# The first two chunks of a hash-attention and MLP kernel in another hand-written order

## The chip, the cores and the metric

The kernel runs on one core of one Trainium2 chip. The metric is the device time of one execution in microseconds (us); a kernel's number is the median of several runs. Engines are named as in the profile: PE (TensorE matmuls), PEld (its weight loads), DVE (VectorE), ACT (ScalarE), POOL (GpSimd) and SP (SyncE, which only issues transfers here). The profile is one execution of its own, with its own span.

## The reference

Each of 4 batches has 8 heads of 768 tokens with 64 dimensions. A query may attend only to keys of its own bucket; the bucket is the pattern of signs of six random projections. The outputs of the 8 heads together are one row of 512 values, which goes through a layer norm and a two-layer MLP.

```python
def _attn_ref(q, k, v, proj):
    q_bits = (np.einsum('bhsd,dk->bhsk', q, proj) > 0)      # six signs per token
    k_bits = (np.einsum('bhsd,dk->bhsk', k, proj) > 0)
    ...
    mask = q_bucket[:, :, :, None] == k_bucket[:, :, None, :]
    scores = scale * np.matmul(q, k.transpose(0, 1, 3, 2))
    scores = np.where(mask, scores, -1000000000.0)
    ...                                                     # softmax over keys
    return np.matmul(attn, v)

def _moe_ref(x, g_ln, w_ch1, w_ch2):
    xn = (x - mu) / np.sqrt(var + 1e-06) * g_ln
    ch = np.maximum(xn @ w_ch1, 0.0) @ w_ch2                # 512 -> 2048 -> 512
    return x + ch
```

## The kernel before

**Masking by matmul.** A head's operand in the tile `slots` has 70 rows: 64 rows of the transposed q or k in bf16 and 6 rows of bits, each plus or minus a constant. One matmul over the 70 rows gives the score plus a term that is largest where all six bits agree; the exponential on ACT (line 409) takes that largest value off again, so keys of other buckets come out as zero.

**Chunks and units.** The work is cut into 12 chunks (4 batches, three chunks of 256 queries each). A chunk's attention is 12 units, three for each of four pairs of heads. A unit is four score matmuls into a PSUM tile `sc` (line 403, two buffers), one ACT exponential of 128x1024 into `ex` (line 409, three buffers) and eight matmuls `av` with the values (line 437, two buffers in PSUM). The third unit of a pair ends with two DVE instructions that divide by the sum of weights (lines 452 and 462). For batch 0 the first `av` of a pair is opened by a small matmul (line 428), and `row_sums` (line 354, evicted at 357) prepares its operand.

**How batch 0 is prepared.** There is nothing to hide its preparation behind except its own attention, so the order of the first two chunks is written out by hand in `first_two` (each engine runs its instructions in the order of the program text there). For each head:
- `transposes(h, a)`, line 211: three f32 transposes on PE of q (a=0) or k (a=1) into a PSUM tile; each covers two token blocks, so that 64 partitions hold the even blocks and 64 the odd ones. Line 219 (DVE, q) and line 221 (ACT, k) evict them to the f32 tile `qkT` (four buffers). The PSUM tile is one of two `mm` buffers; for head 1 it is an `sc` buffer.
- `casts(h)`, lines 226 to 231: two casts of 64x768 from `qkT` to bf16 `slots`, even and odd blocks. Heads 0 and 1: one on POOL and one on ACT. Heads 4 and 6: one on POOL and one on DVE. The others: both on DVE.
- `hash_pair(j, a)`, line 306: projects both heads of pair j in f32; line 311 (DVE) turns the sums into bits. After a=1 it copies the bits to the six rows of `slots`, four copies of 6x768 for each pair: pair 0 two on DVE (326), one on ACT (322) and one on POOL (324), the other pairs three on DVE and one on POOL.

`keep_awake` (line 656) issues dummy matmuls. `values` (line 330) casts the v of four heads on POOL. `load_w1` and `load_w2` (lines 560, 567) and the loads of batch 1 (lines 147, 168) are issued by POOL. `narrow` (line 239) casts batch 1's q and k on POOL, `blocks` (line 244) transposes them on DVE.

The loop over `seq` issues, for step i, first the next unit's scores, then the steps that the table `also` names for i, then the values of unit i. Chunks 0 and 1 alternate by pairs of heads (chunk 0 pair 0, chunk 1 pair 0, chunk 0 pair 1 and so on; the last pairs run chunk 0's pairs 2 and 3 first). All of a pair's bits and casts must be there before its first unit.

**From the third chunk on** nothing is in hand order: `interleave` mixes attention units with the MLP of an earlier chunk (lines 519 `hp` and 536 `o`; the hidden values are evicted to `hbuf` at 129 on DVE or 133 on ACT) and with the preparation of later batches, and a scheduler places the instructions of each engine. Among these are `squares` (line 191), eight ACT instructions for each batch that sum squares of q and k, for a safety check at the end.

Of the kernel before, what the change touches and what calls it, by code (L numbers as in the profile page):

```python
# [9 lines left out]
F32 = mybir.dt.float32  # L10
# [4 lines left out]
AF = mybir.ActivationFunctionType  # L15
# [5 lines left out]
Q_SCALE = 2.0**-12  # L21
# [7 lines left out]
def kernel(  # L29
# [11 lines left out]
    nc = tc.nc  # L41
    P = 128

    B, H, S, D = q.shape
    n_bits = proj.shape[1]
# [10 lines left out]
    scale = 1.0 / math.sqrt(D)  # L56
# [9 lines left out]
    proj1 = consts.tile([P, 2, 32], F32)  # L66
# [25 lines left out]
    HS = HC * P  # L92
# [11 lines left out]
    for i in range(2):  # L104
# [8 lines left out]
    ps_sc = main.enter_context(  # L113
        tc.tile_pool(name="ps_sc", bufs=2, space=bass.MemoryType.PSUM)
    )
    ps_av = main.enter_context(
        tc.tile_pool(name="ps_av", bufs=2, space=bass.MemoryType.PSUM)
    )
# [17 lines left out]
    def load_half(b, half):  # L136

        h0 = half * H // 2
        t = {}
        for nm in "qk":  # L140
            t[nm] = nat.tile([P, H // 2, NC, D], F32, tag=f"{nm}nat", name=f"{nm}nat")

        cuts = [[0, 1, 2, 4] if half == 0 else [0, 2, 4], [0, 4], [0, 2, 4], [0, 2, 4]][b]
        for lo, hi in zip(cuts, cuts[1:]):
            for nm, src in (("q", q), ("k", k)):
                eng = nc.gpsimd if b == 1 else nc.scalar if nm == "k" and hi - lo == 1 else nc.sync
                eng.dma_start(
                    out=t[nm][:, lo:hi],
                    in_=src[b, h0 + lo : h0 + hi].rearrange("h (p c) d -> p h c d", p=P),
                )  # L150
        if b == 0 and half == 0:
            nc.scalar.dma_start(out=proj1[0:D, 0, 0:n_bits], in_=proj)

            nc.scalar.activation(wake2[:, 0:1], wake2[:, 1:2], AF.Exp)
            t["v"] = load_values(b, half)
        return t

    def load_values(b, half):
        h0 = half * H // 2
        eng = nc.gpsimd if (b, half) == (1, 0) else nc.sync  # L160
        if (b, half) == (0, 1):

            t = work.tile([P, NH * CT // 2], F32, tag="h", bufs=1, name="vnat1")[
                :, 0 : H // 2 * NC * D
            ].rearrange("p (h c d) -> p h c d", h=H // 2, c=NC)
        else:
            t = nat.tile([P, H // 2, NC, D], F32, tag="vnat", bufs=1, name="vnat")
        eng.dma_start(
            out=t, in_=v[b, h0 : h0 + H // 2].rearrange("h (p c) d -> p h c d", p=P)
        )  # L170
        return t

    class Prep:

# [6 lines left out]
        def load(self, half):  # L181
            self.tiles[half] = load_half(self.b, half)
# [16 lines left out]

            return self.sl[0:D, h, :, par * HS : (par + 1) * HS]  # L200

        def transposes(self, h, a):

            if a == 0:
                self.qkT[h] = work.tile([P, 2, HS], F32, tag="qkT", bufs=4, name="qkT")
            if h == 1:
                tp = ps_sc.tile([P, 2, 512], F32, tag="sc", name="tpose")[:, 0, 0:HS]
            else:
                tp = ps_mm.tile([P, HS], F32, tag="mm", name="tpose")
            for i in range(HC):  # L210
                nc.tensor.transpose(  # L211
                    tp[:, i * P : (i + 1) * P],
                    self.tiles[h // 4]["qk"[a]][:, h % 4, 2 * i : 2 * i + 2].rearrange(
                        "p c d -> p (c d)"
                    ),
                    identf,
                )
            if a == 0:
                nc.vector.tensor_scalar_mul(self.qkT[h][:, a, :], tp, Q_SCALE)
            else:  # L220
                nc.scalar.activation(self.qkT[h][:, a, :], tp, AF.Copy)

        def casts(self, h):
            src = self.qkT[h]
            if h < 2:
                nc.gpsimd.tensor_copy(self.tokens(h, 0), src[0:D])
                nc.scalar.activation(self.tokens(h, 1), src[D:P], AF.Copy)
            else:
                eng = nc.gpsimd if h in (4, 6) else nc.vector
                eng.tensor_copy(self.tokens(h, 0), src[0:D])  # L230
                nc.vector.tensor_copy(self.tokens(h, 1), src[D:P])  # L231

        def narrow(self, half, a):

# [64 lines left out]
        def hash_pair(self, j, a):  # L299

            if a == 0:
                self.pair_bits = work.tile([P, 2, HS], BF16, tag="bits", name="bits")
            bits = self.pair_bits
            hp = ps_mm.tile([P, HS], F32, tag="mm", name="hash")
            for g in range(4):
                nc.tensor.matmul(  # L306
                    hp[32 * g : 32 * (g + 1), :],
                    proj1[:, g % 2, :],
                    self.qkT[2 * j + g // 2][:, a, :],
                )  # L310
            nc.vector.tensor_scalar(  # L311
                bits[:, a, :], hp,
                scalar1=0.0, scalar2=0.5, op0=AOP.is_gt, op1=AOP.subtract,
            )
            if a == 0:
                return
            for g in range(4):
                par = g % 2
                dst = self.sl[D:K1, 2 * j + g // 2, :, par * HS : (par + 1) * HS]
                src = bits[32 * g : 32 * g + n_bits]  # L320
                if g == 2 and j == 0:
                    nc.scalar.activation(dst, src, AF.Copy)
                elif g == 3:
                    nc.gpsimd.tensor_copy(dst, src)
                else:
                    nc.vector.tensor_copy(dst, src)  # L326

        def values(self, half):
            hs = slice(half * H // 2, (half + 1) * H // 2)
# [234 lines left out]
    def load_w2():  # L564
        w2ap = moe_w_ch2.rearrange("(o p) d -> p o d", p=P)
        for n8 in range(0, NH, NH // 2):
            nc.gpsimd.dma_start(
                out=w2_sb[:, n8 : n8 + NH // 2, :], in_=w2ap[:, n8 : n8 + NH // 2, :]
            )
# [61 lines left out]
    prep = preps[0]  # L631
# [4 lines left out]
    units = {n: att_units(*chunks[n], xs[n]) for n in range(3)}  # L636
    mlp = {0: mlp_steps(*chunks[0], xs[0])}

    def head(h):
        prep.transposes(h, 0)  # L640
        prep.transposes(h, 1)
        prep.casts(h)

    def first_two():

        nxt = preps[1]
        prep.load(0)
        prep.load(1)
        prep.load_v(1)
        block_diagonal()  # L650
        nc.sync.dma_start(out=gbc, in_=moe_g_ln.partition_broadcast(P))

        def keep_awake(n):
            tp = ps_mm.tile([P, P], F32, tag="mm", name="wakep")
            for _ in range(n):
                nc.tensor.matmul(tp, wake, wake)  # L656

        keep_awake(26)
        head(0)
        head(1)  # L660
        nc.vector.tensor_copy(proj1[D : 2 * D, 1, 0:n_bits], proj1[0:D, 0, 0:n_bits])
        keep_awake(3)
        prep.hash_pair(0, 0)
        prep.hash_pair(0, 1)
        keep_awake(10)
        prep.values(0)
        load_w1()
        groups = [(0, 0), (0, 1), (1, 0), (1, 1), (2, 0), (3, 0), (2, 1), (3, 1)]
        seq = [(n, 3 * j + g) for j, n in groups for g in range(3)]

        also = {
            0: [lambda: head(2), lambda: prep.values(1)],
            1: [lambda: prep.row_sums(0), lambda: head(3), lambda: nxt.load(0)],
            3: [lambda: prep.hash_pair(1, 0)],
            4: [lambda: prep.hash_pair(1, 1)],
            5: [lambda: head(4), load_w2],
            6: [lambda: head(5)],
            7: [lambda: prep.hash_pair(2, 0)],
            8: [
                lambda: prep.row_sums(1), lambda: prep.hash_pair(2, 1), lambda: nxt.load(1), lambda: nxt.load_v(0),  # L680
            ],
            9: [lambda: head(6)],
            10: [lambda: head(7)],
            11: [lambda: prep.hash_pair(3, 0)],
            12: [
                lambda: prep.hash_pair(3, 1), lambda: nxt.narrow(0, 0), lambda: nxt.narrow(0, 1),
            ],
            14: [lambda: nxt.blocks(0, 0, 0)],
            15: [
                lambda: nxt.blocks(0, 0, 1),  # L690
            ],
            18: [mlp[0][0][1]],
            19: [lambda: nxt.operands(0)],
            22: [mlp[0][3]],
            23: [mlp[0][1][0][1]],
        }
        units[0][0][0]()
        for i, (n, u) in enumerate(seq):
            m, w = seq[i + 1] if i + 1 < len(seq) else (2, 0)
            units[m][w][0]()  # L700
            for f in also.get(i, []):
                f()
            units[n][u][1]()

    plan = {
        2: "K10 H10 N11 B11 V10 W11 | T11 H11 E10 Q00 L20 V11 W20",
# [21 lines left out]
    with tc.manual_schedule():  # L731
        first_two()
# [211 lines left out]
```

## Time and profile before

| what | us |
|---|---|
| median of three runs (lowest, highest) | 325.96 (324.23, 326.18) |
| span of the profiled execution | 325.2 |
| PE busy in the span | 305.4 |
| ACT, DVE, POOL busy | 216.8, 181.4, 83.8 |
| PE busy in the 259 us from 66 us on | 247.93 |

A start in the timeline is counted from the span's first instruction. Where a group has several instructions ("x3"), the duration is from the start of the first to the end of the last; the bracket gives how long the engine had been idle before it and what ended that. A wait in the chain is put down to what ended last.

The stages of the first 66 us, by the first exponential of each pair of heads in the timeline (line 409):

| pair 0 of chunk 0 | pair 1 | pair 2 | pair 3 | first of the third chunk | first hash of batch 1 (line 275) |
|---|---|---|---|---|---|
| 11.99 | 22.72 | 34.07 | 38.68 | 52.06 | 64.38 |

### The profile page before, as it was taken

How to read it: one execution, taken by the hardware profiler on the slowest of the kernel's cores; microseconds unless marked ns; L12 is line 12 of the kernel's file. 1: busy time of each engine (PE TensorE's matmuls, PEld its weight loads, DVE VectorE, ACT ScalarE, POOL GpSimd, SP SyncE). 2: the span in 40 equal slices, each digit the busy share in tenths (PEclk: the TensorE clock that was granted, in tenths of full speed). 3: DMA queues.
4: the chain of work that ended last, by engine and by line, in shares of the span. 5: the costliest groups of instructions: out<-in, count | busy, mean ns of one | idle time of the engine just before them, and what ended most of it. 6: DMA issues, size and time to landing. Idle time of an engine off the chain costs nothing.

```text
span 325.2 us, 7843 instructions
## 1 busy us (share of the span) xinstructions
PE 305.4 (94%) x3249; PEld 225.9 (69%) x3276; DVE 181.4 (56%) x399; ACT 216.8 (67%) x274; POOL 83.8 (26%) x105
## 2 busy tenths in 40 slices
PE   6888899999999999999999999989999999999991
PEld 5655568767758868858768769759679688685750
DVE  1578974483575695446596674534643735446320
ACT  4567687935685886876976866997667568672110
POOL 4546623744032260056082040200200200201000
PEclk9999967999999999999999999999999999999998
DMA  7999996985289469497444552030020200200201
GB/s 225 366 211 301 208 331 110 214 250 135 63 187 262 109 166 204 90 266 241 80 111 85 71 120 50 1 89 12 19 80 2 65 34 2 65 34 15 87 27 46
DMA packets 64875, 40.94 MB, mean 126 GB/s; under 512 B 47184, under 2 KB 59728, under 8 KB 64832
## 3 DMA queue, kind: packets, MB, share of 16 engines
q1 hardware_dynamic: 60368, 31.85, 39.2%
q0 software_dynamic: 4096, 8.13, 10.5%
q8 instruction: 27, 0.44, 0.6%
q10 hardware_dynamic: 368, 0.39, 0.4%
q14 instruction: 16, 0.13, 0.1%
HBM read 27.98 MB, written 6.88 MB: 107 GB/s over the span
## 4 chain that ended last, share of the span: by engine, by line
PE 81%; ACT 9%; DVE 5%; issue 3%; ACTq 0%; DVEq 0%
PE hp L519 25%; PE o L536 21%; PE sc L403 17%; PE av L437 10%; ACT ex L409 4%; PE hash L275 3%; DVE slots L326 2%; PE hash L306 2%; ACT qnat L191 1%; ACT knat L191 1%; PE tpose L211 1%; PE wakep L656 1%; DVE bits L311 1%; ACT hbuf L133 1%; DVE slots L231 1%
## 5 line engine op out<-in xcount | busy, mean ns | idle before, releaser
L409 ACT ACTIVATE ex<-sc,expb 128x1024 bf16<-128x1024 f32 x144 | 159.7, 1114 | 65.7 <-PE sc L403 65.0
L519 PE MATMUL hp<-xnT,w_sb 128*128 128x256 bf16 x768 | 99.0, 273 | 0.3 <-ACT hbuf L133 0.3
L536 PE MATMUL o<-w_sb,hbuf 128*128 128x512 bf16 x357 | 92.4, 379 | 1.9 <-ACT hbuf L133 0.7
L403 PE MATMUL sc<-slots 70*128 70x256 bf16 x576 | 90.0, 278 | 3.3 <-DVE slots L326 2.9
L519 PEld LDWEIGHTS <-w_sb 128*128 128x128 bf16 x768 | 72.4, 98 | 9.6 <-issue 0.6
L437 PEld LDWEIGHTS <-ex 128*128 128x128 bf16 x1152 | 54.4, 99 | 22.6 <-ACT ex L409 9.3
L403 PEld LDWEIGHTS <-slots 70*128 70x128 bf16 x576 | 52.1, 99 | 17.5 <-DVE slots L326 2.7
L437 PE MATMUL av<-vaug,ex 128*128 128x65 bf16 x1152 | 60.8, 196 | 2.6 <-ACT ex L409 2.4
L129 DVE TENSOR_SCALAR hbuf<-hp 128x512 bf16<-128x512 f32 x45 | 31.0, 688 | 49.2 <-PE hp L519 48.4
L536 PEld LDWEIGHTS <-hbuf 128*128 128x128 bf16 x384 | 35.5, 97 | 29.2 <-issue 1.2
L497 POOL TENSOR_SCALAR rs<-mv 128x2 f32<-128x2 f32 x12 | 6.2, 513 | 168.0 <-DVE mv L482 167.9
L133 ACT ACTIVATE hbuf<-hp 128x512 bf16<-128x512 f32 x51 | 30.4, 596 | 21.6 <-PE hp L519 21.4
L541 DVE SCALAR_TENSOR_TENSOR x<-o,rs,x 128x512 f32<-128x512 f32 x24 | 17.8, 741 | 33.3 <-PE o L536 33.3
L462 DVE TENSOR_TENSOR x<-x,rc 128x256 f32<-128x256 f32 x36 | 20.7, 574 | 1.0
L454 DVE TENSOR_SCALAR rc<-av 128x4 f32<-128x4 f32 x36 | 5.7, 158 | 23.6 <-PE av L437 23.6
L483 DVE SCALAR_TENSOR_TENSOR xn<-x,mv,gbc 128x512 bf16<-128x512 f32 x24 | 18.0, 766 | 0.1
L481 DVE BATCH_NORM_STATS2 stats<-x 128x6 f32<-128x512 f32 x24 | 15.4, 678 | 0.2
L330 POOL CAST vaug<-vnat 128x1536 bf16<-128x1536 f32 x8 | 12.2, 1525 | 10.5 <-DMA vnat<-in_v_dram 5.5
L455 DVE TENSOR_TENSOR x<-av,vsum 128x256 f32<-128x256 f32 x36 | 14.9, 413 | 0.0
L191 ACT ACTIVATE knat<-knat 128x768 f32<-128x768 f32 x16 | 13.5, 848 | 0.0
L191 ACT ACTIVATE qnat<-qnat 128x768 f32<-128x768 f32 x16 | 13.5, 844 | 0.0
L239 POOL CAST nat<-qnat 128x1536 bf16<-128x1536 f32 x6 | 9.0, 1501 | 16.7 <-DMA qnat<-in_q_dram 10.7
(79 smaller groups left out, 207.6 us busy)
## 6 DMA issues: line engine op xcount, KB each, us to landing
out_dram<-x SPq DMA_DIRECT2D x24, 256.0 KB
vnat<-in_v_dram SPq DMA_DIRECT2D x7, 768.0 KB
qnat<-in_q_dram SPq DMA_DIRECT2D x11, 384.0 KB
knat<-in_k_dram SPq DMA_DIRECT2D x11, 384.0 KB
w_sb<-in_moe_w_ch_dram POOLq DMA_DIRECT2D x4, 1024.0 KB, 13.7
slots<-slots SPq DMA_DIRECT2D x6, 384.0 KB
qnat<-in_q_dram POOLq DMA_DIRECT2D x2, 768.0 KB, 13.3
knat<-in_k_dram POOLq DMA_DIRECT2D x2, 768.0 KB, 14.6
```

The lines of the kernel that those rows point to most:

```text
L129: nc.vector.tensor_scalar_max(dst, src, 0.0)
L133: nc.scalar.activation(dst, src, AF.Relu if relu else AF.Copy)
L191: nc.scalar.activation(src, src, AF.Square, accum_out=sq[:, a, col : col + 1],)
L403: nc.tensor.matmul(sc[:, i, :], sl[0:K1, h, 1, kj * P : (kj + 1) * P], sl[0:K1, h, 0, q0 : q0 + CT],)
L409: nc.scalar.activation(ex, sc, AF.Exp, bias=expb[:, 1:2] if b else expb[:, 0:1], scale=scale if b else scale / Q_SCALE,)
L437: nc.tensor.matmul(av[:, h - ha, qi, :], state[g][:, i, qi * P : (qi + 1) * P], va[:, h, CMAP[b][kj], :], start=(b > 0 and (g, i, qi) == ( ...
L462: nc.vector.tensor_tensor(xv, num, rc.unsqueeze(3).to_broadcast([P, 2, TT, D]), op=AOP.mult)
L481: nc.vector.bn_stats(stats, x[:, i, :])
L483: nc.vector.scalar_tensor_tensor(xn[:, :, i, :], x[:, i, :].rearrange("p (o d) -> p o d", d=P), mv[:, i, 0:1], gbc.rearrange("p (o d) -> p ...
L519: nc.tensor.matmul(hp[:, i, :], w1_sb[:, dt, nt * P : (nt + 1) * P], st["xnT"][:, dt, :], start=(dt == 0), stop=(dt == ND - 1),)
L536: nc.tensor.matmul(o2, st["h"][:, nt, i * P : (i + 1) * P], w2_sb[:, nt, :], start=(nt == 0), stop=(nt == NH - 1),)
L541: nc.vector.scalar_tensor_tensor(x[:, i, :], o2, st["rs"][:, i : i + 1], x[:, i, :], op0=AOP.mult, op1=AOP.add,)
```

## The change

- The transfer of `proj` is issued by SP, behind head 0's q, and not by ACT behind both k loads. The values of heads 0 to 3 come as two transfers (heads 0 and 1 ahead of q and k of heads 2 and 3, heads 2 and 3 behind them), and the POOL cast of them as two, `pair_values`.
- `keep_awake(3)` and `keep_awake(10)` go; the 26 dummy matmuls at the start stay.
- `casts` becomes `cast` with an engine for each half. Heads 2 to 7: all on DVE. Head 0: DVE and ACT. Head 1: POOL and ACT, as before.
- The four bit copies become a step of their own, `bit_rows`, all on DVE.
- The transposes of heads 2 and 3 stand before the first scores, into an `sc` and the two `av` buffers, evicted by ACT and DVE (head 2 both by ACT). Those of heads 4 and 5 stand at steps 4 and 5, with their casts at 6 and 7; those of heads 6 and 7 at 9 and 10. Before, each head's transposes and casts were one step.
- `values(1)`, batch 1's loads, `load_w2`, `row_sums(1)`, `narrow` and `blocks` keep their order among themselves and move by zero to two steps.

From the end of `seq` on, PE has the same instructions in the same order in both kernels, and DVE and POOL too. In the third chunk the order on ACT and SP differs. ACT before: `hbuf`, square of q, exponential, `hbuf`, square of q, `hbuf`, square of k, `hbuf`, exponential, `hbuf`, square of k, `hbuf`, exponential. ACT after: `hbuf`, both squares of q, exponential, square of k, `hbuf`, square of k, `hbuf`, `hbuf`, exponential, `hbuf`, `hbuf`, exponential. On SP one load of batch 2's q stands ahead of the second transposing transfer of batch 1, not behind it.

```diff
+            if (b, half, hi) == (0, 0, 1):
+                nc.sync.dma_start(out=proj1[0:D, 0, 0:n_bits], in_=proj)
+            if (b, half, hi) == (0, 0, 2):
+                t["v"] = load_values(b, half, 0, 2)
         if b == 0 and half == 0:
-            nc.scalar.dma_start(out=proj1[0:D, 0, 0:n_bits], in_=proj)
-
             nc.scalar.activation(wake2[:, 0:1], wake2[:, 1:2], AF.Exp)
-            t["v"] = load_values(b, half)
+            load_values(b, half, 2, 4, t["v"])
...
-        def transposes(self, h, a):
+        def transposes(self, h, a, space="mm", eng=None):
...
-        def casts(self, h):
-            src = self.qkT[h]
-            if h < 2:
-                nc.gpsimd.tensor_copy(self.tokens(h, 0), src[0:D])
-                nc.scalar.activation(self.tokens(h, 1), src[D:P], AF.Copy)
-            else:
-                eng = nc.gpsimd if h in (4, 6) else nc.vector
-                eng.tensor_copy(self.tokens(h, 0), src[0:D])
-                nc.vector.tensor_copy(self.tokens(h, 1), src[D:P])
+        def cast(self, h, par, eng):
+            copy_by(eng, self.tokens(h, par), self.qkT[h][par * D : (par + 1) * D])
...
+        def bit_rows(self, j, engs="VVVV"):
+
             for g in range(4):
                 par = g % 2
                 dst = self.sl[D:K1, 2 * j + g // 2, :, par * HS : (par + 1) * HS]
-                src = bits[32 * g : 32 * g + n_bits]
-                if g == 2 and j == 0:
-                    nc.scalar.activation(dst, src, AF.Copy)
-                elif g == 3:
-                    nc.gpsimd.tensor_copy(dst, src)
-                else:
-                    nc.vector.tensor_copy(dst, src)
+                copy_by(engs[g], dst, self.pair_bits[32 * g : 32 * g + n_bits])
...
+        T, C, B = prep.transposes, prep.cast, prep.bit_rows
         keep_awake(26)
-        head(0)
-        head(1)
+        T(0, 0)
+        T(0, 1)
+        T(1, 0, "sc")
+        T(1, 1, "sc")
+        C(0, 0, "V")
+        C(0, 1, "A")
+        C(1, 0, "G")
+        C(1, 1, "A")
         nc.vector.tensor_copy(proj1[D : 2 * D, 1, 0:n_bits], proj1[0:D, 0, 0:n_bits])
-        keep_awake(3)
+        prep.pair_values(0)
         prep.hash_pair(0, 0)
         prep.hash_pair(0, 1)
-        keep_awake(10)
-        prep.values(0)
+        T(2, 0, "sc", "A")
+        T(2, 1, "sc", "A")
+        B(0)
+        T(3, 0, "av", "V")
+        T(3, 1, "av", "A")
+        prep.pair_values(1)
         load_w1()
...
-            0: [lambda: head(2), lambda: prep.values(1)],
-            1: [lambda: prep.row_sums(0), lambda: head(3), lambda: nxt.load(0)],
-            3: [lambda: prep.hash_pair(1, 0)],
-            4: [lambda: prep.hash_pair(1, 1)],
-            5: [lambda: head(4), load_w2],
-            6: [lambda: head(5)],
-            7: [lambda: prep.hash_pair(2, 0)],
-            8: [
-                lambda: prep.row_sums(1), lambda: prep.hash_pair(2, 1), lambda: nxt.load(1), lambda: nxt.load_v(0),
-            ],
-            9: [lambda: head(6)],
-            10: [lambda: head(7)],
-            11: [lambda: prep.hash_pair(3, 0)],
-            12: [
-                lambda: prep.hash_pair(3, 1), lambda: nxt.narrow(0, 0), lambda: nxt.narrow(0, 1),
-            ],
-            14: [lambda: nxt.blocks(0, 0, 0)],
-            15: [
-                lambda: nxt.blocks(0, 0, 1),
-            ],
+            0: [lambda: C(2, 0, "V"), lambda: C(2, 1, "V")],
+            1: [lambda: C(3, 0, "V"), lambda: C(3, 1, "V"), lambda: prep.row_sums(0)],
+            2: [lambda: prep.hash_pair(1, 0), lambda: prep.values(1)],
+            3: [lambda: prep.hash_pair(1, 1), lambda: B(1), lambda: nxt.load(0)],
+            4: [lambda: T(4, 0), lambda: T(4, 1)],
+            5: [lambda: T(5, 0), lambda: T(5, 1), lambda: load_w2()],
+            6: [lambda: C(4, 0, "V"), lambda: C(4, 1, "V")],
+            7: [lambda: C(5, 0, "V"), lambda: C(5, 1, "V"), lambda: prep.hash_pair(2, 0)],
+            8: [lambda: prep.hash_pair(2, 1), lambda: B(2), lambda: prep.row_sums(1), lambda: nxt.load(1), lambda: nxt.load_v(0)],
+            9: [lambda: T(6, 0), lambda: T(6, 1)],
+            10: [lambda: T(7, 0), lambda: T(7, 1), lambda: C(6, 0, "V"), lambda: C(6, 1, "V")],
+            11: [lambda: C(7, 0, "V"), lambda: C(7, 1, "V"), lambda: prep.hash_pair(3, 0)],
+            12: [lambda: prep.hash_pair(3, 1), lambda: B(3)],
+            13: [lambda: nxt.narrow(0, 0), lambda: nxt.narrow(0, 1)],
+            15: [lambda: nxt.blocks(0, 0, 0)],
+            16: [lambda: nxt.blocks(0, 0, 1)],
```

## The prediction

> **What bounds the kernel now.** First the page: busy times, the slices, the chain.
>
> ```profile
> PE 305.4 (94%) x3249; PEld 225.9 (69%) x3276; DVE 181.4 (56%) x399; ACT 216.8 (67%) x274; POOL 83.8 (26%) x105
> ...
> PEclk9999967999999999999999999999999999999998
> ...
> PE 81%; ACT 9%; DVE 5%; issue 3%; ACTq 0%; DVEq 0%
> ```
>
> PE is the bound of the whole, and the ACT and DVE links of the chain (14%) are where time can go. The windows table (columns: busy time and instructions of PE, PEld, DVE, ACT, POOL, then granted clock) says where:
>
> ```profile
> 4.97:8.39 3.42, 1.57 (x17) 1.34 (x19) 1.18 (x3) 2.54 (x4) 1.64 (x2) 1.00 0.97 290
> ...
> 35.69:39.11 3.42, 3.08 (x43) 1.80 (x36) 2.98 (x5) 2.61 (x3) 2.02 (x2) 1.00 1.24 208
> 39.11:42.52 3.41, 2.09 (x29) 1.41 (x28) 3.03 (x5) 2.89 (x4) 2.00 (x2) 1.00 1.19 281
> 42.52:45.93 3.41, 3.33 (x33) 2.40 (x34) 2.66 (x6) 2.51 (x3) 0.00 (x0) 0.50 1.02 379
> ...
> 66.00:325.00 259.00, 247.93 (x2624) 183.96 (x2648) 140.78 (x321) 170.58 (x215) 50.52 (x58) 1.00 0.38 95
> ```
>
> From 66 us on PE is busy for 247.93 of 259 us, and the change leaves PE's order there alone. So a lead won before the first hash of batch 1 (64.38) moves the end by as much, and nothing else does. Then the timeline of the first 60 us, for waits:
>
> ```profile
> 7.93 0.17 DVE L661 COPY proj<-proj 64x6 f32<-64x6 f32 x1 [1.72 <-DMA proj<-in_proj_dram]
> 7.97 1.67 PE L306 MATMUL hash<-qkT,proj 128*32 128x384 f32 x16 [1.85 <-ACT slots L227]
> ...
> 10.40 0.93 POOL L324 COPY slots<-bits 6x768 bf16<-6x768 bf16 x1 [2.46 <-DVE bits L311]
> ...
> 11.61 0.72 PE L403 MATMUL sc<-slots 70*128 70x256 bf16 x5 [0.33 <-DVE slots L326]
> ...
> 17.64 1.47 POOL L330 CAST vaug<-vnat 128x1536 bf16<-128x1536 f32 x1 [3.02 <-DMA vnat<-in_v_dram]
> 17.67 1.85 DVE L231 CAST slots<-qkT 64x768 bf16<-64x768 f32 x1
> ...
> 36.99 2.79 DVE L326 COPY slots<-bits 6x768 bf16<-6x768 bf16 x3
> ...
> 53.38 0.60 ACT L133 ACTIVATE hbuf<-hp 128x512 bf16<-128x512 f32 x1 [0.20 <-PE hp L519]
> ...
> 55.69 0.60 ACT L133 ACTIVATE hbuf<-hp 128x512 bf16<-128x512 f32 x1
> ```
>
> Three things: the first hash waits for the transfer of `proj`; a DVE cast of 0.55 us takes 1.85 beside a POOL cast, and three bit copies of 0.35 take 2.79 beside POOL's copy and the first `narrow` cast (38.10, 1.47): the two engines hold each other up. And six exponentials, 6.5 us of ACT (3.24 for three), take 10.73 us for pair 0 and 11.35 for pair 1.
>
> **The change part by part.** Leads are against the first exponentials 11.99, 22.72, 34.07, 38.68.
>
> *Start.* `proj` was issued on ACT at 1.67 and had landed by 7.93. On SP it goes out second, near 1.2; head 1's q, issued in that place before, was on PE at 5.02. The hash then waits for DVE: head 1's q evicted at 6.22, the new cast 0.55, the `proj` copy 0.17, so 7.0 and not 7.97. From its start to its last bits were 2.29 us (7.97 to 9.06+1.20): 9.3. Two copies at 0.35 make 10.0 for the first scores; on PE the hash (1.67) and the 12 transposes put in front (four groups, 0.34 apart) also end at 10.0. The second scores need all four copies, 10.7. On ACT the three evictions of heads 2 and 3 end near 10.7. The exponential is then at 10.8. POOL's `pair_values` casts (half of 1.47 each) may hold a copy: 0.3. So 11.1, a lead of 0.9; bounds 1.2, and 0 if `proj` lands no sooner. The split of v puts 0.39 MB ahead of heads 2 and 3, 1.4 us at the 290 GB/s of that window. Their transposes are due near 8.7; before, they ran at 12.05 with no wait for data, so the trace only says that 0 to 2 us of it may show; I take 0, since ACT and DVE have 0.7 to spare there.
>
> *The 13 dummy matmuls.* PE's own time for them, 0.33 and 0.72, stood in waits for DVE: nothing gained. For the clock: the window 4.97 to 8.39 holds the first three, its PE was busy for 1.57 us, and the clock stayed full; without them the hash moves into it, about 2.3. Nothing, then; if the clock were halved for three windows there, 10.24 us as at 42.52, up to 3 us, which is what I find for that below. The Trainium skill (TensorE: Matmul & The Clock Gate, What's actually happening) has the clock halved only after an idle window of about 3.4 us, and by that, too, dropping them costs nothing, as the gap left is under 2 us.
>
> *Pair 1.* Before: head 3's casts held to 19.52, hash, bits to 21.0, copies to 22.66, scores 22.34. Now the transposes are done, and DVE runs from 11.1: eviction 0.56, four casts 2.2, free at 13.9. The hash stands behind chunk 1's first scores, which need the `sc` buffer of the second exponential (12.2 to 13.3) and the 0.69 of `row_sums`: 14.5. The second hash follows one unit later, 0.79+0.33+0.44: 16.1. Its bits end 1.5 later, two copies: 18.3, exponential 19.0. The cast of v for heads 4 to 7 falls right there (its data landed at 17.64) and can hold a copy for 1.3; the issue of batch 1's loads by POOL follows it. I take 20.0, a lead of 2.7; bounds 3.7 and 1.5.
>
> *Pair 2.* PE's work per pair is 6 x (0.44+0.33), two hashes 1.58, four groups of transposes 1.35 and row sums 0.69: 8.2. DVE's is 1.1+2.2+1.1+1.4+1.2 = 7.0 now, up by 0.9 from the copy and cast that POOL had. What made 11.35 of that is that `mm` has two buffers: the second hash waits for DVE to evict the first's bits, behind the casts. That stands: step 7 issues head 5's casts ahead of the hash. No change; bounds 1.1 each way, the 1.1 being the longest POOL hold of one cast before (33, 1.08). Lead 2.7.
>
> *Pair 3.* Before, the copies lost 2.79-1.05 = 1.7. POOL has no bit copies left, so `narrow` no longer waits for 38.03 but runs when batch 1's data land: issue 19.05 and 19.82 plus 13.3 and 14.6, so 32.4 to 34.4. Pair 3's casts and copies are then at 31 to 36. Two narrow casts hold at most 3.0 us: 1.3 more than before; none, 1.7 less. I take 0.4 lost, as the times overlap. Lead 2.3.
>
> *Third chunk.* ACT stood back to back there: from the first `hbuf` (53.38) to the next 2.31. Now it is 0.49 + two squares at 0.82 + exponential 1.0 + square 0.82 = 3.95. The fourth `hp` group (56.34) waits for that buffer: 1.64 lost, less where the half clock makes the `hp` later (1.53 for eight, not 1.03, twice): 0.6. I take 0.7. SP's swap costs nothing: the load waits for squares that are now earlier, and the bits behind it had landed by 75 for scores at 91.19.
>
> *The clock.* Half from 42.52 to 52.76, behind the window in which PE was busy least (2.09). From 42.47 to 49.91 five units took 1.49 each, not 1.08: 2.0; transposes and `hp` add 1.0: a price of 3.0. The stretch that is only attention stays, so I keep it: zero.
>
> Sum: -2.3+0.7 = -1.6. The profiled execution has 325.2, the median is 0.8 above it: 323.6 and **324.4**. Own range of this case 322.8 to 326.0.
>
> **The rivals.**
> *Full clock throughout.* If the window of 2.09 came from the stall of the copies, and pair 3 is earlier, no window need fall so low; each unit there still has 0.77 of PE in 1.08 (71%, against 61% in that window and 90% in the one before). Price: -3.0 of before, less the ACT wait, which rises from 0.7 to 1.6: -2.1 on top, 322.3. By the Trainium skill's rule named above this would happen, since no window is idle; the trace does not bear it out, as 42.52 shows. Chance 0.18.
> *DVE becomes the bound.* `narrow`, the v cast and POOL's DMA issues hold copies that now all are DVE's: the high bounds of pairs 1 and 3 (+1.2, +0.9) eat the lead: 324.4+2.1 = 326.5. Chance 0.17.
> *A second halving, the slower side.* The squares leave PE idle for up to 2.1 us in one window near 52 to 55: busy under 1.4 of 3.4, less than the 2.09 that came before the halving. If that halves the clock for 10.24 us where PE is the bound, half of it is lost: +5.1, so 329.5. It decides if PE's busy time in a window there falls below 2.09. Against it: 1.57 at 4.97 brought none. Chance 0.12.
> *The change does not do what it says:* the instruction order shows the copies and casts on DVE and the third chunk moved on ACT and SP alone. Left out.
>
> **How the numbers follow.** 0.53 for the forecast. Range 321.6 to 328.0: it leaves out half of the second halving and the edge of the full clock. One per cent (322.7, 329.2) is what a measurement here can tell from no change. Faster: 0.7 of the full-clock case and 0.12 of the forecast, 0.19. Slower: 0.6 of the second halving and a little of DVE's, 0.09. Same: 0.72.
>
> **What would show it.** First hash near 7.0; first exponentials near 11.1, 20.0, 31.4, 36.4; `narrow` near 33 with DVE copies over 1 us beside it; the second ACT `hbuf` 3 to 4 us after the first; half clock in one stretch of 10.24 us. Wrong would be a lead lost by 64.38 with no half clock to blame, or a changed busy share after it.

## The result, and the profile after

The changed kernel takes 327.75 us (median of 20 executions, 324.17 to 329.91), the kernel before 325.93 beside it (20 executions, 322.94 to 328.2). The ratio is 1.0071, with a 95% interval of 1.0043 to 1.01: slower by 0.7%, where 0.5% less was forecast. The execution profiled of the changed kernel was the slowest of its twenty (329.91, span 328.0), so places are read from its trace, and sizes from medians.

From the page: busy times, the clock by slices, the chain by engine.

```profile
PE 308.1 (94%) x3236; PEld 227.2 (69%) x3263; DVE 181.1 (55%) x406; ACT 217.0 (66%) x274; POOL 77.4 (24%) x99
...
PEclk9799957799999999999999999999999999999998
...
PE 80%; ACT 8%; DVE 5%; issue 3%; DMA 2%; SPq 0%; ACTq 0%; DVEq 0%
```

The slices show a fall of the clock in the second one, where there was none, and a longer fall from the sixth on; and a DMA has come into the chain. In order of time the chain says which one: it opens with head 1's q.

```profile
1.82 5.06 DMA qnat<-in_q_dram
8.67 2.89 PE hash L319 x16
```

The windows table, cut along the clock's own windows of 3.41 us (busy time and instructions of PE, PEld, DVE, ACT, POOL; then granted clock, DMA share, GB/s):

```profile
5.27:8.69 3.42, 1.31 (x9) 0.71 (x8) 1.36 (x4) 0.49 (x1) 0.00 (x0) 1.00 1.02 338
8.69:12.10 3.41, 3.41 (x19) 1.48 (x19) 1.08 (x3) 2.06 (x3) 2.53 (x4) 0.50 1.03 368
...
36.00:39.41 3.41, 2.05 (x29) 1.36 (x27) 3.20 (x11) 1.77 (x2) 0.00 (x0) 1.00 1.23 203
39.41:42.82 3.41, 3.21 (x30) 2.07 (x28) 2.08 (x3) 2.61 (x4) 0.00 (x0) 0.50 1.26 216
49.65:53.06 3.41, 3.41 (x28) 2.80 (x27) 0.69 (x1) 1.98 (x3) 0.00 (x0) 0.50 1.29 114
56.47:59.89 3.42, 1.56 (x15) 1.39 (x15) 3.03 (x5) 3.42 (x8) 3.42 (x3) 1.00 0.65 141
59.89:63.30 3.41, 3.41 (x25) 2.54 (x23) 0.00 (x0) 1.79 (x3) 3.17 (x6) 0.50 1.10 233
67.50:328.00 260.50, 249.52 (x2657) 185.03 (x2682) 141.76 (x321) 170.77 (x216) 50.57 (x58) 1.00 0.37 94
```

Three times a window in which PE was busy for 1.31 to 2.05 us is followed by half clock: for one window, for four (39.41 to 53.06, three before), and for one. From the first hash of batch 1 on nothing has changed (95.8% busy, before 95.7%), so all of the loss lies in front of it. The timeline there:

```profile
6.92 0.55 PE L227 MATMUL tpose<-identf,qnat 128*128 128x128 f32 x3 [1.46 <-DMA qnat<-in_q_dram]
...
8.13 0.55 PE L227 MATMUL tpose<-identf,knat 128*128 128x128 f32 x3 [0.65 <-DVE qkT L237]
...
8.60 2.96 PE L319 MATMUL hash<-qkT,proj 128*32 128x384 f32 x16
...
32.49 1.47 POOL L252 CAST nat<-knat 128x1536 bf16<-128x1536 f32 x1 [0.49 <-DMA knat<-in_k_dram]
...
32.64 3.43 DVE L183 CAST slots<-qkT 64x768 bf16<-64x768 f32 x4
...
37.59 1.49 DVE L183 COPY slots<-bits 6x768 bf16<-6x768 bf16 x4
...
37.99 0.67 PE L415 MATMUL sc<-slots 70*128 70x256 bf16 x4 [1.35 <-DVE slots L183]
...
57.69 0.59 ACT L133 ACTIVATE hbuf<-hp 128x512 bf16<-128x512 f32 x1
...
58.33 1.03 PE L531 MATMUL hp<-xnT,w_sb 128*128 128x256 bf16 x8 [1.91 <-ACT hbuf L133]
```

| start, us | pair 0 | pair 1 | pair 2 | pair 3 | third chunk | hash of batch 1 |
|---|---|---|---|---|---|---|
| before | 11.99 | 22.72 | 34.07 | 38.68 | 52.06 | 64.38 |
| forecast | 11.1 | 20.0 | 31.4 | 36.4 | | |
| after | 14.65 | 22.79 | 33.24 | 38.76 | 52.45 | 67.46 |

Head 1's q reaches PE at 6.92 (before 5.02), and the start is late by 2.7 us. Pairs 1 and 2 win all of it back and 0.8 more. Pair 3's four casts take 3.43 us beside a `narrow` cast, its scores wait 1.35 us for the copies behind them, and the lead is gone. The third chunk loses 2.7 more: the `hp` group that waits 1.91 us for ACT, and the half clock behind that wait.

### The profile page after: what moved, and what is told of

The parts are those of the page before. It is cut to its first block, busy times and chain, and to the rows that moved or that the text cites. A ratio compares the mean times of both kernels' runs of the same rounds, so it can differ in the third digit from the quotient of the medians.

```text
span 328.0 us, 7800 instructions
## 1 busy us (share of the span) xinstructions
PE 308.1 (94%) x3236; PEld 227.2 (69%) x3263; DVE 181.1 (55%) x406; ACT 217.0 (66%) x274; POOL 77.4 (24%) x99
## 3 DMA queue, kind: packets, MB, share of 16 engines
q0 software_dynamic: 4096, 8.13, 10.9%
## 4 chain that ended last, share of the span: by engine, by line
PE 80%; ACT 8%; DVE 5%; issue 3%; DMA 2%; SPq 0%; ACTq 0%; DVEq 0%
PE hp L531 25%; PE o L548 20%; PE sc L415 17%; PE av L449 10%; ACT ex L421 4%; PE hash L288 2%; PE hash L319 2%; ACT qnat L203 2%; DVE slots L183 2%; ACT knat L203 2%; DMA qnat<-in_q_dram 2%; PE tpose L227 1%; DVE bt L257 1%; ACT hbuf L133 1%; DVE bits L324 1%
## 5 line engine op out<-in xcount | busy, mean ns | idle before, releaser
L531 PE MATMUL hp<-xnT,w_sb 128*128 128x256 bf16 x768 | 100.5, 276 | 1.9 <-ACT hbuf L133 1.9
L531 PEld LDWEIGHTS <-w_sb 128*128 128x128 bf16 x768 | 72.9, 99 | 11.3 <-issue 2.0
L449 PEld LDWEIGHTS <-ex 128*128 128x128 bf16 x1152 | 55.2, 100 | 22.5 <-ACT ex L421 9.6
L449 PE MATMUL av<-vaug,ex 128*128 128x65 bf16 x1152 | 61.5, 197 | 2.6 <-ACT ex L421 2.5
L342 POOL CAST vaug<-vnat 128x1536 bf16<-128x1536 f32 x7 | 10.7, 1533 | 14.3 <-DMA vnat<-in_v_dram 9.5
```

The lines of the kernel that those rows point to most:

```text
L449: nc.tensor.matmul(av[:, h - ha, qi, :], state[g][:, i, qi * P : (qi + 1) * P], va[:, h, CMAP[b][kj], :], start=(b > 0 and (g, i, qi) == ( ...
L531: nc.tensor.matmul(hp[:, i, :], w1_sb[:, dt, nt * P : (nt + 1) * P], st["xnT"][:, dt, :], start=(dt == 0), stop=(dt == ND - 1),)
```

## The experiments

A median here stands beside the kernel before on the same chip (325.4 to 326.2 in the five sets). Executions of one kernel scatter by up to 8 us, so differences under 0.5 us are read from traces, not medians.

**First set: undo one part.** `proj` back on ACT (e1); the third chunk's ACT order of before, forced (e2); both (e3); the kernel before with the changed order (e4).

```diff
-            if (b, half, hi) == (0, 0, 1):
-                nc.sync.dma_start(out=proj1[0:D, 0, 0:n_bits], in_=proj)
...
         if b == 0 and half == 0:
+            nc.scalar.dma_start(out=proj1[0:D, 0, 0:n_bits], in_=proj)
```

> The changed kernel with one thing put back: the transfer of proj is issued by ACT behind both k loads, as in the kernel before. Theory A (proj on SP made head 1's q late, and the lost start is what the end pays for): head 1's q transposed near 5.0 and not 6.9, first hash near 8.0 and not 8.6, first exponential near 11.8 and not 14.65, pair 1 some 2 to 2.7 us earlier than 22.79, and the time 1.5 to 2.7 us below the changed kernel's 327.75, about 325.5. Rival B (pair 1 hangs on something that comes at a fixed time, the values' transfer or POOL's casts): the first exponential moves, pair 1 stays at 22.8, and the time stays within 0.7 us of 327.75. Rival C (the halved clock at 8.7 and not the transfer made the start late): the q comes back to 5.0, but the clock is halved near 8 all the same and the first exponential is not before 13.5.

> The changed kernel with one thing put back: in the third chunk ACT's first fourteen instructions stand in the order of the kernel before (each square behind one hbuf eviction), by edges that fix the issue order alone. Theory (the squares ahead of the second hbuf cost what the traces differ by between the second hbuf and the first hash of batch 1): second ACT hbuf 2.3 us behind the first and not 4.0, no wait of 1.9 us of PE for hbuf, first hash of batch 1 about 13.7 us behind the first hbuf's start less what the half clock gives back, and the time 1.5 to 2 us below the changed kernel's 327.75: 326.0. Rival (the hp groups wait for the halved clock anyway, and the order is worth nothing): second hbuf earlier, first hash of batch 1 less than 0.5 us earlier, time within 0.5 us of 327.75.

> Both put back at once: proj on ACT and the third chunk's ACT order; what is left of the change is the transposes a pair ahead, the casts and bit copies on DVE, the split values and the dummy matmuls. If both theories hold and add up: 327.75 - 2.2 - 1.7 = 323.9, about 2 us below the kernel before (325.93). If the lost start is absorbed by pair 1 (rival B): about 326. If the DVE-only casts and copies themselves cost time: above 326 even so.

> The kernel before with the changed kernel's ACT order in the third chunk, and nothing else of the change. Theory (the order costs by itself): second ACT hbuf 4 us behind the first, PE waits near 2 us for it, first hash of batch 1 near 66 and not 64.4, and the time 1.5 to 2 us above the kernel before's 325.93: 327.6. Rival (it costs only where the clock is full and the lead is already lost): within 0.5 us of 325.93.

Measured: e1 327.7 (ratio to the kernel before 1.0062, interval 1.0024 to 1.01), e2 326.99 (0.9988, 0.9929 to 1.0047), e3 326.16 (1.001, 0.9972 to 1.0047), e4 326.4 (0.9989, 0.9942 to 1.0036). The start came back in e1 as theory A said (q at 5.24, first exponential 11.36, pair 1 at 19.78, pair 2 at 30.51, 2.7 us earlier than in the change), and the median gained nothing. e2 gained 0.8 where its theory had 1.5 to 2, e3 stayed 2.3 above the 323.9 of its sum, and e4 is 0.2 above the kernel before, as its rival had it. Where the lead went stands in e1's timeline and windows:

```profile
29.91 4.63 DVE L182 CAST slots<-qkT 64x768 bf16<-64x768 f32 x4
...
30.36 1.47 POOL L251 CAST nat<-qnat 128x1536 bf16<-128x1536 f32 x1 [6.21 <-DMA qnat<-in_q_dram]
...
32.32 1.80 POOL L251 CAST nat<-knat 128x1536 bf16<-128x1536 f32 x1 [0.50 <-DMA knat<-in_k_dram]
...
36.45 1.04 PE L414 MATMUL sc<-slots 70*128 70x256 bf16 x4 [2.54 <-DVE slots L182]
```

```profile
32.54:35.95 3.41, 1.37 (x25) 1.02 (x21) 3.36 (x6) 1.76 (x2) 1.58 (x1) 0.98 1.25 208
35.95:39.36 3.41, 2.91 (x26) 2.24 (x27) 2.83 (x8) 1.59 (x2) 0.00 (x0) 0.50 1.23 202
```

The `narrow` casts run when batch 1's data land, 30.4 us, whatever the lead. Pair 3's casts, now 2.7 us earlier, meet both of them, not one: 4.63 us, not 3.43. PE waits 2.54 us, its window falls to 1.37, and the clock is halved until 49.6. None of the three theories stated for e1 had this; it became theory D.

**Second set: hold `narrow` back.** One POOL copy of 6x2 elements that reads what DVE's last bit copy of pair 3 wrote, ahead of `narrow`: alone (f1); with e3's two parts (f2). Beside them the 13 dummy matmuls put back (f3), and everything together with an `sc` buffer each for head 1's q and k (f4).

```diff
+        def hold_pool(self, j):
+            last = self.sl[D:K1, 2 * j + 1, :, 2 * HS - 1 : 2 * HS]
+            nc.gpsimd.tensor_copy(held[D : D + n_bits], last)
...
-            13: [lambda: nxt.narrow(0, 0), lambda: nxt.narrow(0, 1)],
+            13: [lambda: prep.hold_pool(3), lambda: nxt.narrow(0, 0), lambda: nxt.narrow(0, 1)],
```

> The changed kernel with one instruction more: ahead of the first narrow cast POOL copies 6x2 elements of what DVE's last bit copy of pair 3 wrote, so that no narrow cast can run beside pair 3's casts and copies. Theory D (narrow beside DVE's casts and copies makes pair 3 late, and the PE wait there, 1.35 us in the changed kernel, 2.54 and 2.29 in the two runs with proj on ACT, lowers PE's busy time in one window to 1.1 to 2.1 us and brings the long halving of the clock): the four casts of pair 3 take 2.2 to 2.4 us and the four copies 1.4 to 1.5, each beside no narrow; pair 3's first exponential at most 5 us behind pair 2's and not 5.5 to 7; no halving in front of 50 us; time 2 to 4 us below the changed kernel's 327.75. Rival (the wait moves to another place, or the clock is halved all the same by the start or by pair 2): pair 3 comes sooner, but a halving of three or more windows stays and the time is within 1 us of 327.75.

> Three parts put back or mended at once: proj on ACT, the third chunk's ACT order of the kernel before, and narrow held behind pair 3's copies. Theory D with the lead of the start: first exponentials near 11.4 to 13.3, pair 3's about 5 us behind pair 2's, no long halving in most executions, time 323 or below, which is under the 326.16 of the same kernel without the hold. Rival: 326, as without the hold.

> The changed kernel with the 3 dummy matmuls ahead of pair 0's first hash and the 10 behind its second put back; by itself this brings the third chunk's ACT order of the kernel before back, too, so it stands beside the run with that order alone (326.99). Theory (the missing 13 let the clock fall at 8 to 9 us, or stay low from the start as in the run with both parts put back, where the tensor engine worked at half pace until 10.4 us): the first hash takes 1.6 to 1.7 us, first exponential near 13, time 1 to 2 us below 326.99. Rival (the gap that matters is the 1.5 us in which PE waits for head 1's q, ahead of any of the 13): first hash still 2.7 us or more, first exponential not before 14, time within 0.7 us of 326.99.

> Five parts at once: proj on ACT, the third chunk's ACT order of the kernel before, narrow held, the 13 dummy matmuls, and head 1's q and k each in an sc buffer of their own, as before (in the changed kernel they share one, and PE waited 0.65 us for q's eviction before it could transpose k). What is left of the change: the casts and bit copies of pairs 1 to 3 on DVE and the transposes a pair ahead. If each part costs what the theories say: first exponential near 11.5, no halving in most executions, time 322 to 323.5, below both kernels. If the casts and copies on DVE cost time of their own: 325 or above.

Measured: f1 324.73 (0.997, 0.9928 to 1.0013), f2 321.05 (0.9851, 0.9792 to 0.9909), f3 326.88 (1.0007, 0.9974 to 1.004), f4 321.14 (0.9844, 0.9799 to 0.9888; its six executions between 320.47 and 321.48). Theory D holds: one POOL instruction is worth 3.0 us in the change (f1 beside the change) and 5.1 beside e3's parts (f2 beside e3). f4's timeline shows the casts and copies clear of `narrow`:

```profile
30.44 2.25 DVE L184 CAST slots<-qkT 64x768 bf16<-64x768 f32 x4
...
34.20 1.48 DVE L184 COPY slots<-bits 6x768 bf16<-6x768 bf16 x4
...
34.61 0.67 PE L421 MATMUL sc<-slots 70*128 70x256 bf16 x4 [0.17 <-DVE slots L184]
...
35.84 0.18 POOL L340 COPY held<-slots 6x2 bf16<-6x2 bf16 x1 [11.15 <-DVE slots L184]
...
36.08 1.46 POOL L253 CAST nat<-qnat 128x1536 bf16<-128x1536 f32 x1
```

The casts take 2.25 us, the scores wait 0.17, and no window of f4's first 70 us is at half clock. f3 misses its theory: the hash still took 2.65 us and the first exponential stood at 14.97, as the rival had it.

**Third set: single parts where the clock is quiet.** The kernel before with the hold (g1); f4 with `proj` on SP (g2), with the changed ACT order (g3), without the 13 dummies (g4). The edits are those above.

> The kernel before with the hold alone: POOL reads what DVE's last bit copy of pair 3 wrote ahead of the first narrow cast. Theory D (it is the narrow casts beside DVE's work that make pair 3 late and bring the long halving, in either kernel): pair 3's three bit copies on DVE take 1.1 to 1.8 us and not 2.79, the window that had 2.09 us of PE fills up, the halving goes in most executions, and the time falls from 326 to 321.5 to 323.5. Rival (what the run with five parts gains, 321.14, comes from the casts and copies that DVE alone does, a pair ahead): the kernel before gains at most 1 us from the hold and stays near 325.

> The run with five parts (321.14, its executions between 320.47 and 321.48), but with proj on SP ahead of head 1's q, as in the change. If head 1's q, 1.5 to 2 us late, is on the path that sets the end: head 1's q transposed near 6.5, first exponential 1.5 to 2.7 us later, time 322.6 to 323.8. Rival (pair 1 absorbs it, as the run with proj alone put back suggested, 327.7 and no gain): time within 0.5 us of 321.14.

> The run with five parts, but with the changed kernel's ACT order in the third chunk. The forecast's term was 0.7, and 1.64 where the clock is full, as it should be here: 321.8 or 322.8. What the kernel before with that order showed (326.4 beside 326.2; its executions at the full clock 323.7 beside 323.2): 321.3 to 321.7, because the hp groups that follow run back to back and get the wait back.

> The run with five parts, but without the 13 dummy matmuls. The forecast's term was nothing, and up to 3 us if the clock fell at the start. Theory (PE's busy time in the window around 5 to 8.6 us falls to where the half pace sets in or stays on, in a part of the executions): half of the executions 1 to 2 us later, the median 321.5 to 322.5, a wider spread. Rival (nothing, as forecast, since the gaps at the start are mostly closed by the other parts): within 0.3 us of 321.14 and the same spread.

Measured: g1 322.8 (0.9923, 0.9892 to 0.9954), g2 322.41 (0.9935, 0.9898 to 0.9972), g3 321.04 (0.9871, 0.9836 to 0.9907), g4 321.16 (0.9882, 0.9835 to 0.993). So the kernel before paid for `narrow` too, 2.6 us here: theory D holds in both kernels. In the kernel before it is mostly the clock that is won: pair 3 stands 4.61 us behind pair 2 with the hold and without it, but 79 of 115 executions of the kernel before had a mean clock under 0.986, and of g1's 12 one. Half of the rival holds too, since f4 stays 1.7 us below g1 and g4, in the same set, 1.6 (the intervals of g1 and g4 overlap, those of g1 and f4 just do not). That is what the rest of the change is worth: the transposes a pair ahead, the casts and copies on DVE and the split values, which no run takes apart. `proj` on SP costs 1.3 us here; the 13 dummies nothing; the ACT order nothing in the median, though g3's trace shows it: from pair 2's first exponential to the first hash of batch 1 26.86 us, in f4 26.41.

**The wait or the clock?** e3 with 40 dummy matmuls where PE waits for pair 3's copies, `narrow` not held.

```diff
             units[n][u][1]()
+            if i == 13:
+                keep_awake(40)
```

> The run with proj on ACT and the third chunk's ACT order put back (326.16), narrow not held, and 40 dummy matmuls more (0.055 us each at full clock, 2.2 us) where PE waited 2.29 us for pair 3's copies. Theory (idle PE in that wait is what the halving of 37.5 to 51.2 us follows): copies as slow as before (over 3 us for four) and pair 3 as late, but PE busy for over 3 us in each window there, no halving of three or more windows, and the time lower by what the half clock cost, about 3 us: 323 to 323.5, with 2 us left to the run with narrow held (321.05). Rival (the halving comes from something else, DMA or the casts, and idle PE only stands beside it): halved all the same, time 326 or above.

Measured: 323.69 (0.995, 0.9912 to 0.9987), 2.5 us below e3, or 2.2 when each is taken against the kernel before beside it. Of e3's 12 executions 11 had a mean clock under 0.986, of these 12 two. e3's windows first, then those of this run:

```profile
34.12:37.53 3.41, 1.12 (x22) 0.95 (x21) 3.30 (x8) 1.40 (x2) 0.40 (x1) 1.00 1.23 202
37.53:40.94 3.41, 3.41 (x29) 2.39 (x28) 2.99 (x7) 2.23 (x2) 0.00 (x0) 0.50 1.22 213
```

```profile
32.82:36.24 3.42, 3.42 (x57) 2.38 (x54) 3.35 (x8) 2.39 (x3) 0.17 (x1) 1.00 1.24 208
36.24:39.65 3.41, 3.01 (x49) 2.63 (x46) 2.63 (x8) 1.49 (x3) 0.00 (x0) 1.00 1.22 197
39.65:43.06 3.41, 2.89 (x44) 1.97 (x45) 2.17 (x5) 3.41 (x5) 0.00 (x0) 1.00 1.21 210
```

The casts are still slow (3.44 us beside a `narrow`) and the scores still late, but PE is busy and the clock stays full there: idle PE brings the halving, as the theory said. So the 5.1 us of the hold are about 2.5 of clock and 2.6 of wait (a little less of wait, since the dummies ended 0.8 us behind the first copy, the one that the scores wait for, and held the scores themselves).

**Last set: which part of the start?** The change with `narrow` held (f1) and one part put back: `proj` on ACT (i1), the ACT order (i2), the dummies (i3), `proj` on SP behind head 1's q (i4):

```diff
-            if (b, half, hi) == (0, 0, 1):
+            if (b, half, hi) == (0, 0, 2):
                 nc.sync.dma_start(out=proj1[0:D, 0, 0:n_bits], in_=proj)
```

> The changed kernel with narrow held (324.73) and proj on ACT behind both k loads. Theory (proj's place makes head 1's q late, and the idle PE behind that keeps or brings the half pace at the start): 321.0 to 321.8, nearly all of the 3.7 us. Rival (the ACT order is what costs): 323.5 or above.

> The changed kernel with narrow held (324.73) and the third chunk's ACT order of the kernel before, proj left on SP. Theory: within 0.5 us of 324.73, first exponential still after 13.5 us. Rival: 322.5 or below.

> The changed kernel with narrow held (324.73) and the 13 dummy matmuls put back, its ACT order kept and proj left on SP. If the 13 matter where the q is late (they lie in the window behind the wait for it): 322.4 to 323.3, as in the run with five parts and proj on SP (322.41), and fewer executions with a halved clock. Rival (they stand behind the wait, too late to fill it): within 0.5 us of 324.73.

> The changed kernel with narrow held (324.73) and proj on SP behind head 1's q, not ahead of it. If the place in the queue is all that matters: head 1's q on PE near 5.0, first hash near 7 to 8, and the time as with proj on ACT, 321.0 to 321.8. Rival (the transfer is late wherever SP issues it behind two loads of q, and the hash waits for it): first hash after 8, time 322.5 or above.

Measured: i1 322.21 (0.9884, 0.9817 to 0.9951), i2 321.63 (0.9862, 0.98 to 0.9924), i3 325.08 (0.9958, 0.9911 to 1.0004), i4 322.44 (0.9855, 0.9788 to 0.9921). The dummies change nothing again. i4 answers its question: with the same transfer on the same queue, one place later, head 1's q is on PE at 4.93 and the first exponential at 11.08.

```profile
4.93 0.55 PE L229 MATMUL tpose<-identf,qnat 128*128 128x128 f32 x3
```

The medians of i1 and i4 are 0.4 and 0.6 above the 321.8 that bounded their theories; three of i4's six executions had a mean clock under 0.986. i2 goes against its theory, which had no gain. With `narrow` held, medians over all kernels of this study that differ in nothing but dummies and head 1's buffer:

| | changed ACT order | ACT order of before |
|---|---|---|
| `proj` on SP, ahead of q | 324.8 (f1, i3: 24 executions) | 322.3 (g2, i2: 18) |
| `proj` on ACT | 321.4 (g3, i1: 12) | 321.1 (f2, f4, g4: 18) |

Either part put back alone gives most of the 3.7 us, so the two do not add: 1.2 or 3.4 us for `proj`, 0.3 or 2.5 for the order. A part of that is the clock: 8 of the 24 executions in the first cell had a mean clock under 0.986, in the other three 3 of 48. The executions with 0.99 or more average 323.9 and 322.0 us in the first row, 321.5 and 320.8 in the second, which is nearer to a plain sum.

The traces of the change and its variants show one place of loss that the hold does not touch. At pair 1 the four bit copies take 1.49 to 3.04 us, beside POOL's cast of v or its DMA issues. They take 2.69 or more in seven of the sixteen traces (among them i3 and i4); in six of these seven the clock is then halved for one or two windows, and pair 2 stands 12.2 to 15.1 us behind pair 1. In the other ten it stands 10.3 to 11.3 behind. No run holds POOL back there, so the cause is argued from the overlap, and what it adds to the medians stays open.

## Why the prediction was wrong

The time lay in the range, but the direction was wrong: 1.6 us less was forecast, 1.8 more measured. With `narrow` held in both kernels the change is still the slower one (f1 324.73, g1 322.8; 1.4 us when each is taken against the kernel before beside it), since the hold gives 3.0 us in the change and 2.6 in the kernel before. So the direction was set by the place of `proj` and the order on ACT, 3.7 us together with `narrow` held; `narrow` and the clock are why undoing them alone gains little (e1 nothing, e3 1.6). By its own steps:

- *Start* (lead 0.9, bounds 1.2 and 0) failed in sign. The step took `proj` ahead in SP's queue and kept head 1's q at the 5.02 of the old trace, though that q now stood behind it. Over the traces the first exponential is at 13.6 to 15.9 in the seven kernels of the change with `proj` ahead of the q, and at 11.1 to 13.3 in the nine where it isn't; the medians with `narrow` held differ by 1.2 to 3.4 us. In the profile after PE waited for the q, and the hash for what came behind it: it starts at 8.60, not near 7.0. The rest of the step was right: i4, with the q at 4.93, has the hash at 6.60 and the first exponential at 11.08, where 11.1 was forecast. The shared `sc` buffer of head 1's q and k, a wait of 0.65 us that I had not listed, shows no cost: f2 has it and g4 doesn't, 321.05 and 321.16.
- *The 13 dummy matmuls* (nothing) was right: f3 beside e2, g4 beside f4, i3 beside f1 differ by 0.1, 0.0 and 0.4 us. A window at the start was halved, as the bound allowed, but for one window, and behind PE's wait for the q, which the dummies do not fill.
- *Pair 1* (8.9 us from the first exponential) measured 8.14; *Pair 2* (11.35, no change, bound 1.1) measured 10.45. Both gained a little more than forecast, and f4 repeats them: 8.13 and 10.44. Pair 2's step had the second hash wait for DVE; in the profile after it follows the first by 1.57 us (before 2.26) and waits for nothing of DVE's.
- *Pair 3* (0.4 lost) had the mechanism, `narrow` beside DVE, and mis-sized it: 0.9 was lost in the profile after (5.52 us behind pair 2, before 4.61) and 2.5 in e1 (7.08), beyond its bound of 1.3. It set the 1.7 us that the copies lost before against the new loss, but those were hardly on the path: in g1 the copies take 1.64 us and pair 3 stands at 4.61 all the same, and clear of `narrow` in f4 at 4.33. What was hit now were the casts ahead of the copies (2.25 us clear, 3.43 with one `narrow` beside them, 4.63 with two), and the better the lead, the more of `narrow` they meet. And it had no term for the clock: the wait empties a window, and in e3 the halving behind that cost as much again (h1: 2.5 us). The Trainium skill (SBUF — State Buffer, SBUF: two separate sides) has GpSimd share a port pair with VectorE instructions in modes that use two ports, by a lock that the first to start holds for its whole instruction while the other is blocked. The 4.63 beside 2.25 agrees with blocking; whether these casts run in such a mode no trace here shows.
- *Third chunk* (0.7, and 1.6 at full clock by the rival) had the mechanism: in the profile after the second `hbuf` starts 3.97 us behind the first (3.95 forecast) and PE waits 1.91. Its worth at full clock is half of that price: with `narrow` held and no halving in between, pair 2's first exponential to the hash of batch 1 takes 26.1 to 26.4 us in five kernels of the change with the old order and 26.8 to 27.4 in four with the new one, 0.8 apart. The medians of the table say 0.3 or 2.5.
- *The clock* (zero) took one profile's stretch as fixed, and it is not. Of 115 executions of the kernel before, 34 had a mean clock of 0.99 or more and took 323.3 us on average, and 79 had less than 0.986 and took 326.6. That difference, 3.2, bears out the price of 3.0. But the change did not meet the halving more often: 12 of its 20 executions were under 0.986, and they took 327.9 on average, the seven with 0.99 or more 327.5. So the recorded mean clock does not explain why the change is slower than the kernel before; at 0.99 or more it is slower by 4.2. It does go with the lost lead: of e1's 12 executions all were under 0.986, of the 18 of f2, f4 and g4 none.

Of the rivals, *DVE becomes the bound* had the mechanism of pair 3 and the right side (326.5, measured 327.75), but its other half, pair 1, did not come in the profile after (8.14, not 10.1). *The second halving* came, behind a window of 1.56 as its rule had it, but for one window. *Full clock throughout* (322.3) is near what f2 and f4 come to, 321.1, but only with `proj`, the order and `narrow` put right. A gain is there behind these three: f4 is 1.7 us below g1. That this is the size of the forecast's 1.6 is chance, since that sum had 0.9 for the start in it and 0.7 against it for the order.

## What to carry to other kernels

Follow a won lead to the first instruction whose time is set by a transfer and not by the program: what was clear of it may now run beside it, as DVE's casts did with POOL's here, and a lead of 2.7 us left the median where it was. A small transfer moved one place ahead in a queue made the load that it passed late (q on PE at 6.1 to 6.9 us in the seven traces, not 4.8 to 5.4); one place later it did not. And a wait of 2.3 us cost 5.1 where it emptied a clock window (e3 beside f2), so price a stall with PE's busy time in the window around it, over several executions.

## What the runs showed of the hardware

- Half clock follows windows in which PE is far from idle: busy for 1.12 (e3), 1.20 and 1.45 (e2), 1.31, 1.56 and 2.05 (after), 1.37 (e1), 2.09 (before) and 2.19 us of 3.41 (e4). It lasts one window, two (e2, behind 1.45) or three to four, though PE is then busy for 2.9 us or more of each. Other windows of 1.50 and 2.13 (e1) and 1.57 us (before) brought none, so busy time alone is not the whole rule. The Trainium skill (TensorE: Matmul & The Clock Gate, What's actually happening) names an idle window as the condition; the runs here need less than that.
- At the start PE works at about 0.6 of its later pace with a granted clock of 1.00 in the records: in e3's timeline three transposes took 0.85 to 0.90 us until 7.8 and the hash 2.71; in e1 from 5.2 us on three transposes took 0.49 to 0.55 and the hash 1.60. The end of it moved from trace to trace and lies near the end of a window (5.23 in e1, 10.22 in e3). The Trainium skill (TensorE: Matmul & The Clock Gate, What's actually happening) says that the window runs freely and does not begin with the kernel; the clock's windows lie 1.6 us apart between e1 (5.23) and e3 (6.81), which agrees. These are e3's lines, and the row of its windows table:

```profile
6.92 0.90 PE L227 MATMUL tpose<-identf,knat 128*128 128x128 f32 x3 [0.65 <-DVE qkT L237]
7.75 2.71 PE L319 MATMUL hash<-qkT,proj 128*32 128x384 f32 x16
10.39 0.55 PE L227 MATMUL tpose<-identf,qnat 128*128 128x128 f32 x3
```

```profile
6.81:10.22 3.41, 3.30 (x19) 1.10 (x19) 1.24 (x4) 2.06 (x3) 1.59 (x2) 1.00 1.02 364
```
